# Linear attention with a SwiGLU layer on one core: the first batch's last 64 rows computed with the third batch's attention, one tile cleared earlier, four loads given to the planner first

## The chip, the core and the metric

The kernel runs on one NeuronCore of a Trainium2 chip. Five engines run their own instruction streams and wait for each other through semaphores: TensorE (PE in the profile, with PEld for its weight loads), VectorE (DVE), ScalarE (ACT), GpSimd (POOL) and SyncE (SP), which here only issues DMAs. The metric is the device time of one execution in microseconds (us), less is better. The kernel before takes 323.86 us in the median of three runs (323.74 to 324.04).

## The reference

```python
def _attn_ref(q, k, v, g_norm):                       # (8, 8, 576, 64): batch, heads, rows, head size
    kv = np.einsum('bhsd,bhse->bhde', k, v)
    out = np.einsum('bhsd,bhde->bhse', q, kv)
    rms = np.sqrt(np.mean(out * out, axis=-1, keepdims=True) + 1e-06)
    return (out / rms * g_norm)

def _moe_ref(x, w_gate, w_val, w_out, rms_g):         # x: (4608, 512), d_ff = 1536
    rms = np.sqrt(np.mean(x * x, axis=-1, keepdims=True) + 1e-06)
    xn = x / rms * rms_g
    g = xn @ w_gate
    return (g / (1.0 + np.exp(-g)) * (xn @ w_val)) @ w_out
```

Attention has no softmax: per head a 64 x 64 matrix k^T v is formed from all 576 rows, and every row of q is multiplied by it. So a row of q needs nothing of the other rows, only its batch's k^T v. The two normalisations are fused into one factor per row and head ("the chain": sums of squares, plain and weighted with the gains, then an inverse root).

## The kernel before

**Tiling.** 576 rows of a batch are four chunks of 128 rows (NC = 4) and a remainder of 64 (REM). The rows of the expert layer are worked on in nine groups of 512: the four chunks of each of the eight batches, and one group made of the eight remainders (`xr`), which comes next to last. A group runs 12 blocks of d_ff (NF = 12), each a gate product with silu on ScalarE and a value product multiplied in by VectorE (`gate_of`, `val_of`), four matmuls of 512 columns each; then 48 matmuls with w_out.

**The front.** The first batch is written out by hand, since nothing hides its latency. TensorE spins on a tile of zeros (`idle`, 18 + 4 matmuls) until k and v have landed; k^T v is formed, chunks 0 and 1 are taken through attention, and the first group's first half (256 of 512 rows) starts. Behind its slots `behind(n)` puts the attention of chunks 2 and 3 and of the remainder, n being the place in `early`. Weights arrive meanwhile in eight blocks, issued by GpSimd (gate and value columns of three blocks of d_ff each, `wg0, wv0, ... wv3`), on the same DMA engines as q, k and v; the first group's half uses them in that order. Behind them in GpSimd's queue stand the casts of q's chunks 2 and 3 and of q's remainder (`cast_main`, `cast_rem`), the loads of the second batch, w_out, and the third batch's k and v.

**The later batches.** Each batch's attention runs beside the expert layer of the group before it. A planner (`Placer`) keeps a list of slots: per group 24 slots of gate and value products in turn, then 16 of w_out; 28 slots of the first group's second half stand ahead, so the second group begins with slot 28. Each piece of work has an engine and an estimated cost in us (0.68 a VectorE reduction, 1.2 a GpSimd square, 0.85 a GpSimd load issue). `put` takes the first slot behind the work it depends on at which the engine's backlog stays within a limit (GpSimd 2.0, VectorE and ScalarE 0.9). A slot takes off what it has room for: GpSimd 0.85 in a gate or value slot, VectorE 0.95 in a gate and 0.3 in a value slot. `at` puts work into a slot without asking. In a slot, the other engines' work is emitted ahead of the slot's own product, in the order in which it was placed, and TensorE's behind it. Every engine runs its stream in that order.

**One attention** (`place_attention`, batches 3 to 8): SP turns q by DMA transposition (`qT_dma`: chunks, then remainder); k^T v on TensorE (`kv_mm`) and its copies on VectorE; the products of the four chunks (`o_heads`) and of the remainder (`o_mm`). For each of the five pieces then: a square and a copy on ScalarE (`sq_`, `outa_`), a weighted square on GpSimd (`wsq`), two reductions on VectorE (`red`: of the plain and of the weighted square); the chain in parts on VectorE, a scaling for each piece on VectorE (`xna_`), and transpositions by DMA on SP (`x_dma`) into the next group's x. "Chunk" below counts these pieces from 0. While the second group runs, the third batch's attention, the folding of the gains into the weights (on VectorE and ScalarE), and the loads of the fourth batch (`loads_kv(3)`, slots 39 to 42) are all placed in it; those loads are put in place after the attention.

**Tiles that matter.** `kvs` holds k^T v of two heads each, with zero blocks off the diagonal; two buffers taken in turn by batch. `qTs` is turned q, likewise two. Where a piece has 64 rows, the other 64 are zeroed once by a memset.

Of the kernel before, what the change touches and what calls it, by code (L numbers as in the profile page):

```python
# [87 lines left out]
def kernel(  # L88
# [17 lines left out]
    NC = 4  # L106
# [28 lines left out]


    ident = consts.tile([128, 128], BF16, name="ident")
    gbc = consts.tile([128, D], FP32, name="gbc")
# [21 lines left out]
    for tile_, rows in ((krT, REM // 2), (vr, REM // 2), (rems[0][0], REM)):  # L160
        for r0 in (rows, 2 * rows) if rows < REM else (rows,):
            nc.vector.memset(tile_[r0 : REM if r0 < REM else 128], 0.0)
    idle = consts.tile([128, MAIN], BF16, name="idle")
    nc.vector.memset(idle, 0.0)  # L164
    nc.vector.memset(diag, 0.0)
# [77 lines left out]
    class Att:  # L243
        def __init__(self, b):
            self.b = b
            self.kv, self.qT = kvs[b % 2], qTs[b % 2]
            if b < 2:
                self.qTj = self.qT.rearrange("p c j t -> p (c j t)").rearrange("p (j c t) -> p j c t", j=NS, c=NC + 1)
            else:
                self.qTj = self.qT.rearrange("p c j t -> p j c t")  # L250
            self.kv_chunks = range(NC + 1)
            self.o, self.outa, self.sq = {}, {}, {}
            self.xT = {}
            self.st = None
# [79 lines left out]
        def qT_dma(self):  # L334
            flat = mains[self.b, 0].rearrange("p c h d -> p (c h d)")
            nc.sync.dma_start_transpose(out=self.qT[:, 0:NC].rearrange("p c j t -> p (c j) t"), in_=flat)
            rem = rems[0][self.b % 2][:REM].rearrange("p h d -> p (h d)")
            return nc.sync.dma_start_transpose(out=self.qT[:, NC, :, 0:REM], in_=rem)

        def o_mm(self, c, pool=None):  # L340
            self.o[c] = o = (pool or att_p).tile([128, H, D], FP32, name={None: "att"}.get(pool, "mm1" if pool is mm1_p else "o2"))
            for j in range(NS):
                nc.tensor.matmul(  # L343
                    o[:, 2 * j : 2 * j + 2, :], lhsT=self.qTj[:, j, c, :], rhs=self.kv[:, j, :, :],
                    start=j == 0, stop=j == NS - 1, skip_group_check=True,
                )
# [14 lines left out]
        def part(self, t, n):  # L361

            if n == NC:
                return t[:, NC]
            return t[:, n // 2 * 2 : n // 2 * 2 + 2, n % 2 : H : 2]
# [11 lines left out]
        def xna_pairs(self, o, js, c0, c1):  # L377
            if not hasattr(self, "xna"):
                self.xna = xna_p.tile([128, NC + 1, H, D], BF16, name="xna")
            h0, h1 = 2 * js[0], 2 * js[-1] + 2  # L380
            nc.vector.tensor_tensor(
                out=self.xna[:, c0:c1, h0:h1], in0=o,
                in1=self.al[:, c0:c1, h0:h1].to_broadcast([128, c1 - c0, h1 - h0, D]), op=OP.mult,
            )

        def o_of(self, c):
            return self.o[c] if c == NC else self.o["main", c].rearrange("p c h d -> p (c h) d")

# [59 lines left out]
        def red(self, c, which):  # L448
            if self.st is None:
                self.st = stat.tile([128, 2, NC + 1, H], FP32, name="st")  # L450
            of = self.sq[c][:, which]
# [4 lines left out]
        def chain_t(self):  # L456
            if not hasattr(self, "al"):
                t = lambda n, dt=FP32, h=H: stat.tile([128, NC + 1, h], dt, name=n)
                self.u, self.r, self.t, self.z, self.nt, self.al = (t(n) for n in ("u", "r", "t", "z", "nt", "al"))
                self.s = stat.tile([128, NC + 1], FP32, name="srow")  # L460
                self.y = t("y", I32)
# [55 lines left out]
        def xna_(self, c, eng, src=None):  # L517
            if not hasattr(self, "xna"):
                self.xna = xna_p.tile([128, NC + 1, H, D], BF16, name="xna")
            if src is None and c < NC:  # L520
# [55 lines left out]
        def x_dma(self, c0, c1):  # L576
# [3 lines left out]
            else:  # L580
                to = xr[:, :, self.b * REM : (self.b + 1) * REM]
                of = self.xna[:REM, c0].rearrange("p h d -> p (h d)")
# [13 lines left out]
    def place_attention(P, b, casts=(), at=0, chain_at=0):  # L596
        a, start = Att(b), at + 2
        V, A = nc.vector, nc.scalar
        N1 = range(NC + 1)
        P.floor = max(P.floor, at)  # L600
# [6 lines left out]
        for c in N1:  # L607
            p = P.psum(0.24, lambda: a.o_mm(NC), kv + qt) if c == NC else main
            s = P.put("ACT", 0.6, lambda c=c: a.sq_(c), [p])
            outs[c] = P.put("ACT", 0.6, lambda c=c: a.outa_(c), [p])  # L610
            if c >= 2:
                P.tiles[-1 if c == NC else c - 4] += [s, outs[c]]
            assert outs[c][1] < start + 2 * NF, (b, outs)
# [4 lines left out]
        for n in range(0, 13, 4):  # L618
            prev = [P.put("DVE", 0.8, lambda n=n: [f() for f in a.chain(0, NC + 1)[n : n + 4]], prev, chain_at)]
        xn = [P.put("DVE", 0.68, lambda c=c: a.xna_(c, V), prev + [outs[c]]) for c in N1]  # L620
        put = [P.put("SP", 0.0, lambda c=c: a.x_dma(*c), [xn[c[1] - 1]]) for c in ((0, 2), (2, 4), (4, 5))]
        return put[2 if b == B - 1 else 1][1] + X_SLOTS
# [274 lines left out]

    steps = {6: (0, 3), 7: (3, 5), 8: (5, 8), 9: (8, 10), 10: (10, 12)}

    def behind(n):  # L900
        if n == 0:
            ps = a.qT_mm(ALL, (2, 3))
            a.qT_out(ps[:, 0:2], P0, 2, V)
            a.qT_out(ps[:, 2:4], P1, 2, V)
        elif n == 1:
            a.qT_out(a.qT_mm(ALL, (NC,)), ALL, NC, A)
        elif n in (2, 3):
            js = (P0, P1)[n - 2]
            a.sqT_(a.oT_mm(js, 2, 4, o2_p), js, 2, 4)
        elif n == 4:  # L910
            a.sqT_(a.oT_mm(ALL, NC, NC + 1, o2_p), ALL, NC, NC + 1)
        elif n == 5:
            a.st = None
            a.stat_pairs(P0, 2, 4, att_p, "att")
            a.stat_pairs(P1, 2, 4, att_p, "att")
        elif n == 6:
            a.stat_pairs(ALL, NC, NC + 1, att_p, "att")
        if n in steps:
            for f in a.chain(2, NC + 1)[slice(*steps[n])]:
                f()  # L920
        if n in (8, 9):
            held[n - 8] = a.o_pairs((P0, P1)[n - 8], 2, 4, att_p, "att")
        elif n == 10:
            held[2] = a.o_pairs(ALL, NC, NC + 1, o2_p, "o2")
        if n in (12, 13):
            i = (12, 13).index(n)
# [3 lines left out]
        if n in (15, 16):  # L930
            i = (15, 16).index(n)
# [30 lines left out]
    casts = ()  # L962
    for b in range(1, B):
        if b == 1:
            end = place_second(P, 9)
# [51 lines left out]
```

## Time and profile before

| | us |
|---|---|
| median of three runs | 323.86 |
| the profiled execution's own time | 323.98 |
| its span in the trace | 322.2 |
| TensorE busy | 313.7 (97%) |
| VectorE busy | 175.4 (54%) |
| ScalarE busy | 142.9 (44%) |
| GpSimd busy | 89.0 (28%) |
| first product of the first group's expert layer | 18.55 |
| second group | 58.8 to 93.2 |

Times in the trace count from the start of the span. A row of the timeline has the start, the time taken (of all merged instructions), the engine, the line of the kernel, the operation, what is written and read, how many instructions, and in brackets how long the engine stood idle just before and what ended that. A row of the chain has start, duration and what. A row of DMA issues has the number of issues, the size of one and the time from issue to landing; queue rows have packets, MB and the packets' time as a share of 16 DMA engines (over 100% where packets overlap). L238 are the spins, L677 the gate and value products, L695 the product with silu, L454 the reductions, L446 the weighted squares.

### The profile page before, as it was taken

The page shows a single profiled execution, that of the slowest core. Times are in us where ns is not written, and L with a number is a line of the kernel's source. Part 1 is how long each engine was busy: PE and PEld are TensorE (multiplying, and loading weights), DVE is VectorE, ACT ScalarE, POOL GpSimd, SP SyncE. Part 2 cuts the span into 40 slices and gives each one's busy share as a digit, 9 for nine tenths or more (in the row PEclk, how much of TensorE's full clock was granted, in tenths as well). Part 3 has the DMA queues.
Part 4 walks back from the last instruction along what each step waited for, and adds up shares of the span by engine and source line. Part 5 has one row for each costly group of instructions (what it writes and reads, how often), then busy time and mean ns, then how long its engine had stood idle before and what let it go on. Part 6 is the DMA issues. An engine that isn't in the chain of part 4 may idle for free.

```text
span 322.2 us, 5618 instructions
## 1 busy us (share of the span) xinstructions
PE 313.7 (97%) x2158; PEld 160.0 (50%) x2158; DVE 175.4 (54%) x394; ACT 142.9 (44%) x267; POOL 89.0 (28%) x110
## 2 busy tenths in 40 slices
PE   5999999999999999999999999999999999999995
PEld 1678866544444444444444444444444444444443
DVE  4558437487938671768176917781678133203410
ACT  1375466486659322932283227422742233223321
POOL 8763330039006700670058005800420000000000
PEclk9999999999999999999999999999999999999999
DMA  8999999959664994598559956798000600040002
GB/s 213 220 200 199 194 221 220 220 146 144 139 162 130 124 162 141 145 122 144 150 160 102 141 149 181 90 136 167 36 1 0 171 35 0 1 110 22 0 33 100
DMA packets 78358, 40.51 MB, mean 126 GB/s; under 512 B 41976, under 2 KB 73852, under 8 KB 78332
## 3 DMA queue, kind: packets, MB, share of 16 engines
q0 software_dynamic: 30672, 14.16, 34.5%
q1 hardware_dynamic: 46176, 25.01, 31.4%
q10 hardware_dynamic: 1484, 0.99, 1.0%
q8 instruction: 17, 0.28, 0.4%
q14 instruction: 9, 0.07, 0.1%
HBM read 37.78 MB, written 9.44 MB: 147 GB/s over the span
## 4 chain that ended last, share of the span: by engine, by line
PE 97%; DVE 1%; ACT 1%; issue 0%
PE mm L677 58%; PE o L712 27%; PE mm L238 3%; PE att L275 2%; PE mm L712 2%; PE att L343 1%; PE o L356 1%; PE att L552 1%; PE mm L291 0%; PE att L356 0%; PE mm L739 0%; PE o L739 0%; PE mm L705 0%; PE att L321 0%; ACT sqT L415 0%
## 5 line engine op out<-in xcount | busy, mean ns | idle before, releaser
L695 DVE TENSOR_TENSOR h<-silu,mm 128x512 bf16<-128x512 bf16 (+1 forms) x120 | 75.6, 631 | 83.0 <-PE mm L677 73.7
L686 ACT ACTIVATE silu<-mm 128x512 bf16<-128x512 f32 (+1 forms) x120 | 66.4, 557 | 84.2 <-PE mm L677 77.1
L677 PE MATMUL mm<-x,wv 128*128 128x512 bf16 (+1 forms) x432 | 99.9, 356 | 0.0
L677 PE MATMUL mm<-x,wg 128*128 128x512 bf16 (+1 forms) x420 | 98.5, 358 | 0.5 <-DVE h L695 0.5
L712 PE MATMUL o<-wo,h 128*128 128x512 bf16 x396 | 90.1, 379 | 0.0
L446 POOL TENSOR_TENSOR sq<-sq,g 128x512 bf16<-128x512 bf16 x30 | 34.3, 1153 | 130.2 <-ACT sq L391 130.1
L677 PEld LDWEIGHTS <-wv 128*128 128x128 bf16 x480 | 46.2, 98 | 45.2
L677 PEld LDWEIGHTS <-wg 128*128 128x128 bf16 x468 | 45.0, 98 | 45.4 <-issue 1.0
L712 PEld LDWEIGHTS <-h 128*128 128x128 bf16 x420 | 40.2, 98 | 46.0 <-DVE h L695 0.2
L728 ACT COPY osb<-o 128x512 f32<-128x512 f32 x33 | 19.2, 586 | 69.1 <-PE o L712 69.1
L454 DVE TENSOR_REDUCE st<-sq 128x8 f32<-128x512 bf16 x60 | 38.4, 677 | 1.8 <-POOL sq L446 1.7
L304 DVE CAST kvs<-att 64x256 bf16<-64x256 f32 x14 | 5.9, 422 | 30.0 <-PE att L275 29.8
L521 DVE TENSOR_TENSOR xna<-outa,al 128x512 bf16<-128x512 bf16 x24 | 15.0, 684 | 0.0
L238 PE MATMUL mm<-idle 128*128 128x512 bf16 x27 | 8.7, 493 | 4.0 <-DVE idle L164 4.0
L677 PE MATMUL mm<-xr,wg 128*128 128x512 bf16 x48 | 12.3, 379 | 0.0
L677 PE MATMUL mm<-xr,wv 128*128 128x512 bf16 x48 | 12.3, 379 | 0.0
L209 POOL CAST main_q<-stg 128x1024 bf16<-128x1024 f32 (+1 forms) x12 | 11.3, 970 | 0.4 <-DMA stg<-in_q_dram 0.4
L391 ACT ACTIVATE sq<-att 128x512 bf16<-128x512 f32 x18 | 11.1, 618 | 0.0
L395 ACT CAST outa<-att 128x512 bf16<-128x512 f32 x18 | 10.9, 604 | 0.0
L834 ACT ACTIVATE wv<-wv,gain 128x384 bf16<-128x384 bf16 x16 | 9.0, 608 | 0.4 <-PE mm L677 0.4
L195 POOL DMA_DIRECT2D vc<-in_v_dram x9 | 7.8, 864 | 1.8 <-PE mm L677 1.8
L238 PEld LDWEIGHTS <-idle 128*128 128x128 bf16 x31 | 3.6, 119 | 8.6 <-DVE idle L164 4.0
(139 smaller groups left out, 195.3 us busy)
## 6 DMA issues: line engine op xcount, KB each, us to landing
out_dram<-osb SPq DMA_DIRECT2D x31, 256.0 KB, 2.6
stg<-in_q_dram SPq DMA_DIRECT2D x6, 1024.0 KB, 6.8
vc<-in_v_dram POOLq DMA_DIRECT2D x7, 512.0 KB, 8.0
kc<-in_k_dram POOLq DMA_DIRECT2D x7, 512.0 KB, 6.2
wg<-in_moe_w_gate_dram POOLq DMA_DIRECT2D x4, 384.0 KB, 15.8
wv<-in_moe_w_val_dram POOLq DMA_DIRECT2D x4, 384.0 KB, 17.1
wo<-in_moe_w_out_dram POOLq DMA_DIRECT2D x4, 384.0 KB, 13.1
out_dram<-osb SPq DMA_DIRECT2D x9, 128.0 KB, 2.3
```

The costliest lines, as they stand in the source:

```text
L209: return copy(out=mains[b, t][:, cs[0] : cs[1], h0:h1, :], in_=staged[b, t].rearrange("p h (c d) -> p c h d", c=NC)[:, cs[0] : cs[1], h0:h ...
L238: nc.tensor.matmul(ps, lhsT=idle[:, :128], rhs=idle[:, : ps.shape[-1]], start=True, stop=True, skip_group_check=True)
L391: nc.scalar.activation(out=self.sq[c][:, 0], in_=self.o_of(c), func=ACT.Square)
L395: nc.scalar.copy(out=self.outa[c], in_=self.o_of(c))
L446: eng.tensor_tensor(out=self.sq[c][:, 1], in0=self.sq[c][:, 0], in1=g2, op=OP.mult)
L454: nc.vector.reduce_sum(out=self.part(self.st[:, which], c), in_=of, axis=AX.X)
L521: return eng.tensor_tensor(out=self.part(self.xna, c), in0=self.outa[c].rearrange("p (c h) d -> p c h d", c=2), in1=self.part(self.al, c). ...
L677: nc.tensor.matmul(ps[:, : c1 - c0], lhsT=w[n][:, s, jj * 128 : (jj + 1) * 128], rhs=x_of(g, s, c0, c1), start=s == 0, stop=s == NS - 1)
L686: nc.scalar.activation(out=sis[g, j][:, c0:c1], in_=ps, func=ACT.Silu)
L695: nc.vector.tensor_tensor(out=hs[g, j][:, c0:c1], in0=sis[g, j][:, c0:c1], in1=v_ps, op=OP.mult)
L712: nc.tensor.matmul(ps, lhsT=hs[g, j][:, t * 128 : (t + 1) * 128], rhs=wo[j // OB][:, j % OB, :], start=j == 0, stop=j == NF - 1)
L728: (eng.copy if eng is nc.scalar else eng.tensor_copy)(out=o, in_=ps)
```

## The change

Four things are changed together.

- `idle` is cleared by VectorE's first memset, ahead of those of `krT`, `vr` and `rems`. The memsets of the two q remainder tiles' unused rows fall away.
- The first batch's remainder is taken out of `behind` (turning, products, sums, chain columns, scaling, turning back), and its load on SP and cast on GpSimd out of the front. The remaining steps for chunks 2 and 3 get other places.
- The remainder is loaded by GpSimd with a cast (`q0r`), behind w_out; SP turns it with the third batch's q (`q0T`); and the third batch's attention has a sixth chunk, `o_mm(5)`, which multiplies it by the first batch's k^T v, kept in a third buffer `kvs[2]`. Squares, reductions, the chain (6 x 8 columns instead of 5 x 8), scaling and a transposition into the first batch's place in `xr` follow as for the other chunks.
- The fourth batch's four k and v loads are put into slots 39 to 42 before the third batch's attention is placed, not after it.

Cut to its core:

```diff
+    idle = consts.tile([128, MAIN], BF16, name="idle")
+    nc.vector.memset(idle, 0.0)
...
-    kvs = [consts.tile([128, NS, 2, D], BF16, name=f"kvs{n}") for n in range(2)]
+    kvs = [consts.tile([128, NS, 2, D], BF16, name=f"kvs{n}") for n in range(3)]
+    q0r = consts.tile([REM, H, D], BF16, name="q0r")
+    q0T = consts.tile([128, NS, 128], BF16, name="q0T")
...
-            self.kv, self.qT = kvs[b % 2], qTs[b % 2]
+            self.kv, self.qT = kvs[b % 2 if b else 2], qTs[b % 2]
+            self.chunks = NC + 1 + (b == 2)
...
+            if self.b == 2:
+                nc.sync.dma_start_transpose(out=q0T[:, :, 0:REM], in_=q0r.rearrange("p h d -> p (h d)"))
             return nc.sync.dma_start_transpose(out=self.qT[:, NC, :, 0:REM], in_=rem)
...
+                q_, kv_ = (self.qTj[:, j, c, :], self.kv) if c <= NC else (q0T[:, j, :], kvs[2])
                 nc.tensor.matmul(
-                    o[:, 2 * j : 2 * j + 2, :], lhsT=self.qTj[:, j, c, :], rhs=self.kv[:, j, :, :],
+                    o[:, 2 * j : 2 * j + 2, :], lhsT=q_, rhs=kv_[:, j, :, :],
...
-        N1 = range(NC + 1)
+        N1 = range(a.chunks)
...
-    load_rem(0, 0)
...
-    G.memset(rems[0][1][REM:], 0.0)
+    G.memset(kvs[0], 0.0)
...
-    cast_rem(0, 0, G)
...
     wo_loads = [load_wo(n) for n in range(NF // OB)]
+    G.dma_start(out=q0r, in_=q[0, :, MAIN:S, :].rearrange("h p d -> p h d"))
+    G.memset(q0T, 0.0)
...
-    steps = {6: (0, 3), 7: (3, 5), 8: (5, 8), 9: (8, 10), 10: (10, 12)}
+    steps = {5: (0, 4), 7: (4, 6), 8: (6, 8), 9: (8, 12)}
...
-        elif n == 1:
-            a.qT_out(a.qT_mm(ALL, (NC,)), ALL, NC, A)
...
-        elif n == 4:
-            a.sqT_(a.oT_mm(ALL, NC, NC + 1, o2_p), ALL, NC, NC + 1)
...
-        elif n == 6:
-            a.stat_pairs(ALL, NC, NC + 1, att_p, "att")
...
-        elif n == 10:
-            held[2] = a.o_pairs(ALL, NC, NC + 1, o2_p, "o2")
...
-        elif n == 15:
-            a.xna_pairs(held[2], ALL, NC, NC + 1)
...
-        elif n == 18:
-            a.xT_mm(ALL, (NC,))
-            for j in ALL:
-                a.xT_out(j, (NC,), A)
...
+    G.memset(qTs[0][:, NC, :, REM:], 0.0)
...
+        if b == 2:
+            for n, f in enumerate(loads_kv(b + 1)):
+                P.at("POOL", 0.85, f, starts[1] + 11 + n)
...
-            for n, f in enumerate(loads_kv(b + 1)):
-                if b == 2:
-                    P.at("POOL", 0.85, f, starts[1] + 11 + n)
-                else:
-                    P.put("POOL", 0.85, f, at=starts[b - 1] + 14)
+            for f in loads_kv(b + 1) if b > 2 else ():
+                P.put("POOL", 0.85, f, at=starts[b - 1] + 14)
```

More of the change, by code (lines that the diff above doesn't have):

```diff
@@ L159 @@
     xr = consts.tile([128, NS, MAIN], BF16, name="xr")
[L160 to L164, printed above, removed]
+    for tile_ in (krT, vr):
+        for r0, r1 in ((REM // 2, REM), (REM, 128)):
+            nc.vector.memset(tile_[r0:r1], 0.0)
     nc.vector.memset(diag, 0.0)
@@ L361, in part @@
         def part(self, t, n):
-            if n == NC:
-                return t[:, NC]
+            if n >= NC:
+                return t[:, n]
             return t[:, n // 2 * 2 : n // 2 * 2 + 2, n % 2 : H : 2]
@@ L378, in xna_pairs @@
             if not hasattr(self, "xna"):
-                self.xna = xna_p.tile([128, NC + 1, H, D], BF16, name="xna")
+                self.xna = xna_p.tile([128, NC + 2, H, D], BF16, name="xna")
             h0, h1 = 2 * js[0], 2 * js[-1] + 2
@@ L449, in red @@
             if self.st is None:
-                self.st = stat.tile([128, 2, NC + 1, H], FP32, name="st")
+                self.st = stat.tile([128, 2, NC + 2, H], FP32, name="st")
             of = self.sq[c][:, which]
@@ L457, in chain_t @@
             if not hasattr(self, "al"):
-                t = lambda n, dt=FP32, h=H: stat.tile([128, NC + 1, h], dt, name=n)
+                t = lambda n, dt=FP32, h=H: stat.tile([128, NC + 2, h], dt, name=n)
                 self.u, self.r, self.t, self.z, self.nt, self.al = (t(n) for n in ("u", "r", "t", "z", "nt", "al"))
-                self.s = stat.tile([128, NC + 1], FP32, name="srow")
+                self.s = stat.tile([128, NC + 2], FP32, name="srow")
                 self.y = t("y", I32)
@@ L518, in xna_ @@
             if not hasattr(self, "xna"):
-                self.xna = xna_p.tile([128, NC + 1, H, D], BF16, name="xna")
+                self.xna = xna_p.tile([128, NC + 2, H, D], BF16, name="xna")
             if src is None and c < NC:
@@ L618, in place_attention @@
         for n in range(0, 13, 4):
-            prev = [P.put("DVE", 0.8, lambda n=n: [f() for f in a.chain(0, NC + 1)[n : n + 4]], prev, chain_at)]
+            prev = [P.put("DVE", 0.8, lambda n=n: [f() for f in a.chain(0, a.chunks)[n : n + 4]], prev, chain_at)]
         xn = [P.put("DVE", 0.68, lambda c=c: a.xna_(c, V), prev + [outs[c]]) for c in N1]
-        put = [P.put("SP", 0.0, lambda c=c: a.x_dma(*c), [xn[c[1] - 1]]) for c in ((0, 2), (2, 4), (4, 5))]
+        put = [P.put("SP", 0.0, lambda c=c: a.x_dma(*c), [xn[c[1] - 1]]) for c in ((0, 2), (2, 4), (4, 5), (5, 6))[: a.chunks - 2]]
         return put[2 if b == B - 1 else 1][1] + X_SLOTS
@@ L915, in behind @@
             a.stat_pairs(P1, 2, 4, att_p, "att")
-        elif n == 6:
-            a.stat_pairs(ALL, NC, NC + 1, att_p, "att")
         if n in steps:
-            for f in a.chain(2, NC + 1)[slice(*steps[n])]:
+            for f in a.chain(2, NC)[slice(*steps[n])]:
                 f()
-        if n in (8, 9):
-            held[n - 8] = a.o_pairs((P0, P1)[n - 8], 2, 4, att_p, "att")
-        elif n == 10:
-            held[2] = a.o_pairs(ALL, NC, NC + 1, o2_p, "o2")
-        if n in (12, 13):
-            i = (12, 13).index(n)
+        if n in (7, 8):
+            held[n - 7] = a.o_pairs((P0, P1)[n - 7], 2, 4, att_p, "att")
+        if n in (11, 12):
+            i = (11, 12).index(n)
             a.xna_pairs(held[i], (P0, P1)[i], 2, 4)
-        elif n == 15:
-            a.xna_pairs(held[2], ALL, NC, NC + 1)
-        if n in (15, 16):
-            i = (15, 16).index(n)
+        elif n in (14, 15):
+            i = (14, 15).index(n)
             a.xT_mm((P0, P1)[i], (2, 3), None if i else o2_p)
```

9 lines of the change are left out of this document (5 added, 4 removed).

## The prediction

> **What bounds the kernel now.** I read the page's busy shares and chain first, then the chain in order of time, then the timeline of the two places that the change touches (the front, and the second group's expert layer, where the third batch's attention runs), last the DMA view by issue and by stretch.
>
> ```profile
> span 322.2 us, 5618 instructions
> PEclk9999999999999999999999999999999999999999
> PE 97%; DVE 1%; ACT 1%; issue 0%
> ```
>
> TensorE's instructions are 97% of the chain that ends last. So a matmul taken out pays its full spacing, unless the data of the next one are late; work on the other engines pays only where it ends such a wait. Two stretches decide. The front and the first half of the first group, from the chain in order of time (start, us, what):
>
> ```profile
> 20.75 0.22 PE att L310 x4
> ...
> 22.72 0.22 PE o L404 x4
> ...
> 24.01 0.08 PE att L429 x4
> ...
> 26.31 0.22 PE o L371 x4
> ...
> 30.59 0.19 PE att L552 x4
> ```
>
> The five small pieces are the first batch's remainder on TensorE (turned, multiplied, its sums, the product, turned back). The page's chain has no gap here, but what TensorE reads comes in just ahead of it. The last two weight blocks, DMA issues with their time to landing, and the instructions that issue and first use the last:
>
> ```profile
> wg<-in_moe_w_gate_dram POOLq DMA_DIRECT2D x1, 384.0 KB, 18.1
> wv<-in_moe_w_val_dram POOLq DMA_DIRECT2D x1, 384.0 KB, 18.7
> 10.56 0.74 POOL L228 DMA_DIRECT2D wg<-in_moe_w_gate_dram  x1 [0.92 <-DMA vc<-in_v_dram]
> 11.96 0.74 POOL L229 DMA_DIRECT2D wv<-in_moe_w_val_dram  x1 [0.66 <-DMA vc<-in_v_dram]
> 30.67 0.33 PEld L677 LDWEIGHTS <-wv 128*128 128x128 bf16 x4
> ```
>
> They land at 10.56 + 18.1 = 28.66 and 11.96 + 18.7 = 30.66; the first weight load from the last block starts at 30.67. The transfers, 2.0 apart, keep pace with TensorE exactly, so at 30.67 there is a second bound beside TensorE.
>
> The other stretch is the one place behind 20 us where the chain leaves TensorE:
>
> ```profile
> 76.95 1.03 PE L677 MATMUL mm<-x,wv 128*128 128x512 bf16 x4
> 77.17 0.69 DVE L454 TENSOR_REDUCE st<-sq 128x8 f32<-128x512 bf16 x1 [0.85 <-POOL sq L446]
> 77.77 0.68 DVE L695 TENSOR_TENSOR h<-silu,mm 128x512 bf16<-128x512 bf16 x1
> 78.50 1.02 PE L677 MATMUL mm<-x,wg 128*128 128x512 bf16 x4 [0.53 <-DVE h L695]
> 97.75 17.27 PE mm L677 x80
> ```
>
> In plain flow a matmul takes 17.27/80 = 0.216, so the gate at 78.50 was due at 76.95 + 4 x 0.216 = 77.81: 0.69 lost. It waits for block 8's product (77.77), which stands on VectorE behind a reduction that waited 0.85 for GpSimd's weighted square. GpSimd is late for this reason:
>
> ```profile
> 70.50 1.15 POOL L446 TENSOR_TENSOR sq<-sq,g 128x512 bf16<-128x512 bf16 x1 [1.17 <-ACT sq L391]
> 71.59 0.94 POOL L195 DMA_DIRECT2D kc<-in_k_dram  x1
> ...
> 75.97 2.27 POOL L446 TENSOR_TENSOR sq<-sq,g 128x512 bf16<-128x512 bf16 x2
> ```
>
> The four issues of the fourth batch's k and v, of which the first is shown, stand among the five squares: from 71.59 to 75.97 is 4.38, less the one square between them 3.23. The planner placed squares and reductions before it knew of them.
>
> **Part 1: the zero tile first.** The spinning matmuls wait for it.
>
> ```profile
> 3.66 0.27 DVE L164 MEMSET idle<- 128x256 uint32 x1
> 3.99 7.45 PE L238 MATMUL mm<-idle 128*128 128x512 bf16 x22 [3.99 <-DVE idle L164]
> ...
> 9.08 1.86 PEld L238 LDWEIGHTS <-idle 128*128 128x128 bf16 x9 [0.28 <-issue]
> 18.55 1.31 PE mm L705 x12
> ```
>
> Ahead of it stand five memsets, the first from 0.91 on. At their head it is done at 0.91 + 0.27 = 1.2, and the 22 spins run from 1.25 instead of 3.99, ending at 8.7 instead of 11.44. The first real products cannot follow at once: GpSimd's waits at 10.56 and 11.96, quoted above, end with the landing of the two halves of v, so TensorE idles from 8.7 to 10.5 and has 0.9 to 0.95 in hand behind it. The memsets that move behind only lose 0.27 and are read by the products alone, some 9 us later.
>
> **Part 2: the remainder out of the front.** TensorE drops 0.22 + 0.22 + 0.08 + 0.22 + 0.19 = 0.93. Its copies, squares and chain columns on VectorE and ScalarE lie beside TensorE and count nothing. With part 1 TensorE would reach the last weight block 1.84 to 1.88 earlier. But the block must have landed. What moves its landing is the transfer that leaves, the remainder of q: 64 x 8 x 256 bytes = 0.131 MB in 512 packets. From the DMA view, SP's queue in the stretch from 16 to 20 us (packets, MB, share of 16 engines) and all packets and GpSimd's queue from 20 to 28 us, between them GpSimd's wait for that transfer, and last the chain's row of the third batch's k^T v:
>
> ```profile
> q1 hardware_dynamic: 548, 0.14, 26.0%
> 19.45 0.61 POOL L216 CAST remq<-rstg 64x512 bf16<-64x512 f32 x1 [1.56 <-DMA rstg<-in_q_dram]
> DMA packets 2158, 1.62 MB, mean 203 GB/s; under 512 B 63, under 2 KB 2157, under 8 KB 2157
> q0 software_dynamic: 2157, 1.61, 130.7%
> 63.26 0.75 PE att L275 x40
> ```
>
> By bytes it held up the weights for 0.131 MB / 203 GB/s = 0.65. By packets: 26.0% of 4 us x 16 engines over 548 is 30 ns each, 512 make 15.5, over 16 engines at 1.307 abreast 0.74. I take 0.70: landing at 29.96. With 0.08 allowed from landing to use (an estimate; the row at 30.67 shows 0.01), the use moves from 30.67 to 30.04: **-0.63**. The earlier blocks move alike and bind less. Bounds: no effect if the freed time goes to other packets (0), the whole 1.84 if the landing is no bound. Below nothing would need the next batch's loads, which GpSimd issues some 2 us earlier since it no longer waits for the remainder and casts it (1.56 + 0.61), to pass the weights on their queue; with them outstanding from 20 us on, the last two blocks still came 2.0 apart, which for 0.393 MB is 197 GB/s, the whole rate. So I exclude it.
>
> The new load of the remainder stands behind w_out in GpSimd's queue (one issue, some 0.7, and 0.7 of DMA time), with a memset behind it. The third batch's k and v queue behind both and are first read at 63.26 (last row), so the whole rest of the first group hides it. On SP one more transposition stands ahead of the first group's stores, which no engine waits for. All this counts nothing; without its cover it would cost its own 1 to 2 us once.
>
> **Part 3: the loads placed first.** By the planner's rule the four loads (0.85 each) fill GpSimd's room of slots 39 to 42 of the joint list; chunk 2's square (1.2) would make its backlog 2.4, over 2.0, and moves from slot 41 to 43; the squares of chunks 3, 4 and 5 follow in 44, 46 and 47, and each weighted reduction after its square. GpSimd then: first load in the 1.17 before chunk 1's square at 70.50, that square to 71.65, three loads (3.23 - 0.94 = 2.29) to 73.9, squares ending 75.1, 76.3, 77.4, 78.6 (1.15 each). VectorE, 0.60 from one to the next when busy (77.17 to 77.77): weighted reduction of chunk 3 at 76.3, block 8's product at 76.9, done at 77.6. The gate is now due at 77.81 + 0.22 (part 4) = 78.03, so it waits for nothing: **-0.69**. Bounds: all of it, or none if VectorE is 0.4 or more later than reckoned, since the same wait then stands again.
>
> **Part 4: the sixth chunk.** Four matmuls, as the fifth's:
>
> ```profile
> 69.11 0.22 PE att L343 x4
> ```
>
> **+0.22**, no cover. On VectorE two reductions and a scaling (3 x 0.60), on ScalarE two copies, on GpSimd one square. VectorE after the gate above: chunk 4's two reductions, block 9's product at 78.7, done 79.4, gate 11 due at 78.03 + 8 x 0.216 = 79.76: 0.36 to spare. Late next is the third batch's transposed x, with the time that a transposition takes to land:
>
> ```profile
> 85.60 1.89 DVE L521 TENSOR_TENSOR xna<-outa,al 128x512 bf16<-128x512 bf16 x3
> x<-xna SPq DMA_TRANSPOSE x2, 3.3
> 93.23 1.03 PE L677 MATMUL mm<-x,wg 128*128 128x512 bf16 x4
> ```
>
> Chunk 3's scaling ended at 87.49. Chunk 4's last reduction comes 0.87 earlier (78.1 instead of 77.77 + 2 x 0.60 = 78.97), but two reductions (1.2) and three weight foldings (0.23 each) come in between: 88.5. Issue at 88.7, landing 3.3 later at 92.0; the group is due at 93.23 - 0.69 + 0.22 = 92.76. It fits by 0.76 where it had 2.3.
>
> **Sum**, on the profiled execution's own 323.98 (span 322.2 and 1.78 around it): -0.63 - 0.69 + 0.22 = -1.10, 322.88. The median of the runs shown is 0.12 below that execution, so 322.75.
>
> **Rivals.** *The weights do not hold TensorE back* (their landing moves by more than 1.8): -1.84 - 0.69 + 0.22 gives 321.55. For it, no idle time is charged to a weight; against it, the landing at 30.66 fits the first use to 0.01. *The stall in the third batch stays*, since VectorE has more to do there: 322.75 + 0.69 = 323.45. For it, the sixth chunk's 1.2 of reductions against 0.36 to 0.44 to spare. *The x of the third batch is late*: each us over the 0.76 costs one; 1 us late is 323.0, 2 us 324.0.
>
> *Slower: the matmul clock falls back in the new idle time.* The granted clock reads full in every slice (the page's second row above), but nine spins' weight loads from 9.08 on take 1.86, 0.21 each, where the spins before them took (9.08 - 3.99)/12 = 0.42: TensorE needed 5.1 us of work to get its full pace. If 8.7 to 10.5 without work undoes that, the front's matmuls double: if it stays down for as long as it first did, 5.1 us, they lose half of it, 2.55; if until the first gates at 18.55, the 7.1 from 11.44 on hold about 4 of matmuls by the chain, and they lose 4; minus the 1.2 by which TensorE would have waited for weights anyway: up to +2.8, 322.75 + 2.8 = 325.55. It decides the sign once more than 1.2 + 1.1 = 2.3 of matmul work runs at half pace. Against it, the gap is 1.8, a third of the 5.1. The Trainium skill (TensorE: Matmul & The Clock Gate, Part 1: The HAM clock gate) has the pace fall back after an idle window of about 3.4 us, counted in windows that run freely; by that rule 1.8 is too short and the time stays at 322.75. No run here shows such a gap yet.
>
> **Chances.** Forecast 0.52 (its own range 322.3 to 323.2), weights no bound 0.10, stall stays 0.20, late x 0.08, clock 0.10. The range is 321.5 to 323.9: it takes in the first rival's time and the stall that stays, and leaves out most of the clock and the worst of the late x. A measurement of this kernel tells about 0.2% (0.65) from no change; the line is 323.2. Faster: 0.50 + 0.10 + 0.04 of the stall in part + 0.03 = 0.67; within 0.2%: 0.24; slower: 0.09, the clock and the far end of the late x.
>
> **What would show it.** Spins from about 1.25; the first twelve products near 10.5, still 0.056 apart (0.11 would be the clock); the first load from the last value block at 30.0, with the small waits for weights on the way; GpSimd's four load issues ahead of chunk 2's square; gate 10 with no gap; x landing about 0.7 before its use. I am wrong if the last block is used before 29.5 or after 30.5, if a wait for a product stands anywhere in the second group, or if the spacing of the front's matmuls doubles.

## The result and the profile after

Beside each other the kernel before took 323.96 us (323.74 to 324.04, six runs) and the changed one 322.66 (322.24 to 323.05, six runs): a ratio of 0.996 with an interval of 0.9948 to 0.9973, faster by 0.40%. A second time, beside its last variants, the changed kernel took 322.49 (322.27 to 322.70, five runs) against 324.15, 0.995 (0.9937 to 0.9962). The profiled execution took 322.91 (span 321.1), 1.07 less than the one before.

The page of the changed kernel, its span, the granted clock by slices of 8 us, and the shares of the chain:

```profile
span 321.1 us, 5589 instructions
PEclk9799999999999999999999999999999999999999
PE 95%; DMA 3%; ACT 0%; issue 0%; POOL 0%; DVE 0%; POOLq 0%
```

Two things are new: the clock of the second slice reads 7, and a DMA has 3% of the chain. Both belong to the front. The timeline of TensorE there, with the last group of the spins' weight loads:

```profile
1.19 6.26 PE L240 MATMUL mm<-idle 128*128 128x512 bf16 x22 [1.19 <-DVE idle L138]
4.05 2.90 PEld L240 LDWEIGHTS <-idle 128*128 128x128 bf16 x14 [0.17 <-issue]
10.35 0.38 PE L294 MATMUL mm<-vc,main_k 128*128 128x128 bf16 x4 [2.90 <-DMA vc<-in_v_dram]
10.68 0.55 PE L294 MATMUL mm<-vc,main_k 128*128 128x128 bf16 x4
```

The spins begin at 1.19; fourteen of the 22 load their weights in the 2.90 from 4.05 on, 0.21 each, and only the eight before are slow. The full pace came after 2.9 us of spinning where it had taken 5.1, so the spins end at 7.45, and TensorE stands idle for 2.90. The first four products at 10.35 take 0.38, the next four at 10.68 take 0.55. The stretches of this time (length, busy us of PE, PEld, DVE, ACT, POOL with their counts, granted clock, DMA share, GB/s):

```profile
10.00:10.50 0.50, 0.15 (x3) 0.15 (x3) 0.07 (x1) 0.08 (x1) 0.00 (x0) 1.00 1.47 201
10.50:11.00 0.50, 0.50 (x10) 0.50 (x9) 0.50 (x1) 0.00 (x0) 0.41 (x1) 0.76 1.44 198
13.00:14.00 1.00, 1.00 (x11) 0.94 (x9) 0.25 (x3) 0.00 (x0) 0.94 (x3) 0.50 1.22 245
14.00:15.00 1.00, 1.00 (x9) 0.68 (x7) 1.00 (x3) 0.65 (x2) 1.00 (x3) 0.91 1.22 242
```

The clock is still full when work returns, falls about 0.4 later, and stays at 0.50 until shortly after 14. By the means, 0.76 over half a us and 0.91 over one, from about 10.76 to 14.18, 3.4 us. The chain in order of time shows what that did:

```profile
19.15 1.31 PE mm L712 x12
...
29.00 7.98 PE mm L684 x72
...
73.21 0.22 PE att L349 x4
73.43 7.77 PE mm L684 x36
81.20 9.71 PE o L719 x45
```

The first gate products start at 19.15, not 18.55: 0.60 later instead of some 0.95 earlier. The last two weight blocks (issues with their time to landing, the instruction that issues the last, the queue of SP in the stretch from 16 to 20 us), and the weight loads around its first use:

```profile
wg<-in_moe_w_gate_dram POOLq DMA_DIRECT2D x1, 384.0 KB, 17.2
wv<-in_moe_w_val_dram POOLq DMA_DIRECT2D x1, 384.0 KB, 17.9
11.81 0.74 POOL L231 DMA_DIRECT2D wv<-in_moe_w_val_dram  x1 [0.38 <-DMA vc<-in_v_dram]
q1 hardware_dynamic: 12, 0.00, 0.4%
29.41 0.64 PEld L684 LDWEIGHTS <-wg 128*128 128x128 bf16 x6
30.06 0.96 PEld L684 LDWEIGHTS <-wv 128*128 128x128 bf16 x8
30.27 1.47 PE L684 MATMUL mm<-x,wv 128*128 128x256 bf16 x12
```

SP's 548 packets of this stretch are down to 12, and the last block lands at 11.81 + 17.9 = 29.71. TensorE's weight load comes 0.35 after it, with no wait in brackets, and the first product at 30.27: in this execution TensorE itself is the bound, because of the slow 3.4 us.

The second group. GpSimd's stream, then TensorE's products around the old stall, and last SP's transposition of the third batch's x with the group that reads it:

```profile
70.06 1.15 POOL L452 TENSOR_TENSOR sq<-sq,g 128x512 bf16<-128x512 bf16 x1 [0.29 <-ACT sq L397]
71.16 0.73 POOL L193 DMA_DIRECT2D kc<-in_k_dram  x1
71.88 0.89 POOL L197 DMA_DIRECT2D vc<-in_v_dram  x1
72.77 0.69 POOL L193 DMA_DIRECT2D vc<-in_v_dram  x1
73.47 4.53 POOL L452 TENSOR_TENSOR sq<-sq,g 128x512 bf16<-128x512 bf16 x4
76.72 1.03 PE L684 MATMUL mm<-x,wv 128*128 128x512 bf16 x4
77.58 1.03 PE L684 MATMUL mm<-x,wg 128*128 128x512 bf16 x4
78.45 1.03 PE L684 MATMUL mm<-x,wv 128*128 128x512 bf16 x4
88.43 1.29 SPq L590 DMA_TRANSPOSE x<-xna  x1
92.25 1.03 PE L684 MATMUL mm<-x,wg 128*128 128x512 bf16 x4
```

All four loads (the first, at 68.82, isn't shown) stand ahead of chunk 2's square, four squares follow in one piece, and the gate at 77.58 comes 0.86 after the value product, with no wait. x, issued at 88.43 and 3.3 on its way, lands at 91.73, 0.52 before its use at 92.25, and holds nothing up.

Where the 1.07 came from, by two marks, the first product with the last weight block and the second group's first product with w_out. In the chain of the kernel before, the second mark is

```profile
82.18 9.71 PE o L712 x45
```

and the first is 30.67. So 0.40 was won up to the first mark (30.67 to 30.27), 0.58 between the marks (51.51 to 50.93), and 0.09 behind them.

### The profile page after: what moved, and what is told of

Its sections match the earlier page's. It is cut to its first block, busy times and chain, and to the rows that moved or that the text cites. A ratio compares the mean times of both kernels' runs of the same rounds, so it can differ in the third digit from the quotient of the medians.

```text
span 321.1 us, 5589 instructions
## 1 busy us (share of the span) xinstructions
PE 313.1 (98%) x2142; PEld 160.3 (50%) x2142; DVE 177.2 (55%) x395; ACT 142.2 (44%) x263; POOL 90.9 (28%) x113
## 4 chain that ended last, share of the span: by engine, by line
PE 95%; DMA 3%; ACT 0%; issue 0%; POOL 0%; DVE 0%; POOLq 0%
PE mm L684 58%; PE o L719 27%; DMA vc<-in_v_dram 3%; PE att L278 2%; PE mm L719 2%; PE mm L294 1%; PE att L349 1%; PE o L362 1%; PE att L558 1%; PE att L362 0%; PE mm L746 0%; PE o L746 0%; PE mm L712 0%; PE att L313 0%; PE att L324 0%; ACT sqT L421 0%
## 5 line engine op out<-in xcount | busy, mean ns | idle before, releaser
L452 POOL TENSOR_TENSOR sq<-sq,g 128x512 bf16<-128x512 bf16 x31 | 35.4, 1150 | 127.6 <-ACT sq L397 127.6
L460 DVE TENSOR_REDUCE st<-sq 128x8 f32<-128x512 bf16 x62 | 39.7, 677 | 0.2
L240 PE MATMUL mm<-idle 128*128 128x512 bf16 x27 | 7.5, 439 | 1.2 <-DVE idle L138 1.2
L719 PE MATMUL mm<-wo,h 128*128 128x512 bf16 x24 | 7.8, 379 | 0.0
```

The costliest lines, as they stand in the source:

```text
L452: eng.tensor_tensor(out=self.sq[c][:, 1], in0=self.sq[c][:, 0], in1=g2, op=OP.mult)
L460: nc.vector.reduce_sum(out=self.part(self.st[:, which], c), in_=of, axis=AX.X)
L719: nc.tensor.matmul(ps, lhsT=hs[g, j][:, t * 128 : (t + 1) * 128], rhs=wo[j // OB][:, j % OB, :], start=j == 0, stop=j == NF - 1)
```

## The experiments

"The time behind the first mark" is a profiled execution's time less its first mark. Before: 323.98 - 30.67 = 293.31; after: 322.91 - 30.27 = 292.64. It tells what happened behind the front. Each kernel's time is the median of its runs. The experiments ran on three chips, on which the kernel before took 324.05 (31 spins, zero tile late, both on the loads), 323.95 (zero tile alone, transfer, sixth chunk, small operation) and 324.15 (the last four), so a difference of 0.1 to 0.2 across them tells nothing.

**More spins, so that TensorE doesn't idle.**

```diff
-    spin(mm1_p.tile([128, MAIN], FP32, name="mm1"), 18)
+    spin(mm1_p.tile([128, MAIN], FP32, name="mm1"), 31)
```

> The changed kernel with 31 spins of the zero tile in place of 18 (and the 4 behind them as before), so that TensorE does not stand idle from 7.4 to 10.35 us. Theory A (the idle stretch lets the matmul clock fall, and the halved matmuls of 10.7 to 14.5 are what makes TensorE late at the last weight block): granted clock 1.00 from 8 to 16 us, first gate near 18.55 - 0.95 = 17.6, first load from the last value block at its landing, about 29.75 instead of 30.06; median 0.3 to 0.6 below the changed kernel's 322.66, about 322.2, with all runs within 0.3 of each other. Theory B (the weights' landing alone sets the early part, as the prediction had it): the clock is restored, but the median stays within 0.15 of 322.66.

322.37 (322.27 to 323.10); the clock of all five runs is at least 0.999. The timeline of the weight loads:

```profile
28.90 0.32 PEld L684 LDWEIGHTS <-wg 128*128 128x128 bf16 x3
29.59 1.21 PEld L684 LDWEIGHTS <-wv 128*128 128x128 bf16 x12 [0.37 <-DMA wv<-in_moe_w_val_dram]
```

With the clock kept, TensorE reaches the last block early and waits for its landing. So the weights are the second bound that the prediction took them for. The first mark is 29.60, the time behind it 292.67, as in the changed kernel: its slow clock cost only what stands ahead of the first mark, here 0.67.

**The zero tile cleared late again.**

```diff
-    idle = consts.tile([128, MAIN], BF16, name="idle")
-    nc.vector.memset(idle, 0.0)
...
+    idle = consts.tile([128, MAIN], BF16, name="idle")
+    nc.vector.memset(idle, 0.0)
```

> The changed kernel with the zero tile cleared behind the other memsets again (parts 2 to 4 of the change alone). Theory A: spins end near 11.1, no idle stretch, no fall of the clock, first gate near 18.4, TensorE would reach the last value block at about 30.67 - 0.93 = 29.7, just at its landing; median about 322.3, so clearing the tile first costs 0.3 or more. Theory B (the earlier start of the front is worth its 0.9 or is free): 322.66 or more, up to 323.2.

322.51 (322.20 to 322.76), between what the two theories expected: nothing is lost without part 1. The weight loads:

```profile
28.10 1.21 PEld L684 LDWEIGHTS <-wg 128*128 128x128 bf16 x12 [0.16 <-DMA wg<-in_moe_w_gate_dram]
30.01 0.99 PEld L684 LDWEIGHTS <-wv 128*128 128x128 bf16 x10 [0.70 <-DMA wv<-in_moe_w_val_dram]
```

TensorE waits 0.70 for the last block even so. What part 1 hands to the front ends in front of a landing that it doesn't move.

**The zero tile cleared first, alone, in the kernel before.** 
```diff
+    idle = consts.tile([128, MAIN], BF16, name="idle")
+    nc.vector.memset(idle, 0.0)
...
-    idle = consts.tile([128, MAIN], BF16, name="idle")
-    nc.vector.memset(idle, 0.0)
```

> The kernel before with the zero tile cleared first and nothing else changed. TensorE is there only 0.01 behind the last weight block, so nothing can be gained. Theory A (the idle stretch sometimes halves the clock for 3.4 us): executions with a granted clock of 0.995 come out 0.4 to 0.9 above the kernel before, 324.4 to 324.9, those with a full clock at 323.7 to 324.1. Theory B (the fall of the clock costs nothing because the weights are waited for anyway): all within 0.2 of the kernel before, 324.0.

324.36 (323.60 to 324.84) against 323.95: no gain. The eleven runs part by the granted clock of the execution: five with 0.993 or 0.994 took 324.36 to 324.55, five of the six others 323.60 to 324.09. The sixth, at 324.84, is the profiled one: in it the last block was first used at 31.57, 0.90 later than before, at full clock. So part 1 by itself gains nothing that these runs show, and loses about 0.5 where the clock falls.

**The four loads placed last again.**

```diff
-        if b == 2:
-            for n, f in enumerate(loads_kv(b + 1)):
-                P.at("POOL", 0.85, f, starts[1] + 11 + n)
...
-            for f in loads_kv(b + 1) if b > 2 else ():
-                P.put("POOL", 0.85, f, at=starts[b - 1] + 14)
+            for n, f in enumerate(loads_kv(b + 1)):
+                if b == 2:
+                    P.at("POOL", 0.85, f, starts[1] + 11 + n)
+                else:
+                    P.put("POOL", 0.85, f, at=starts[b - 1] + 14)
```

> The changed kernel with the fourth batch's loads placed after the third batch's attention again. Theory A (the order of planning took away the 0.69 stall): the wait for a weighted square returns between blocks 7 and 10 of the second group, 0.7 or more with a sixth chunk behind it; median 0.6 to 1.2 above the changed kernel's 322.66, 323.3 to 323.9. Rival (the stall went because work shifted by the earlier front, not because of the order): no wait over 0.2 in the second group, median within 0.2 of 322.66.

323.22 (323.00 to 323.38), 0.56 more than the changed kernel, a little under the range expected. In four of its seven runs the clock fell; at full clock alone the means are 323.09 and 322.36, 0.73 apart. The old stall is back, in VectorE's and TensorE's timeline:

```profile
76.39 0.69 DVE L460 TENSOR_REDUCE st<-sq 128x8 f32<-128x512 bf16 x1 [0.85 <-POOL sq L452]
77.00 0.68 DVE L702 TENSOR_TENSOR h<-silu,mm 128x512 bf16<-128x512 bf16 x1
77.73 1.02 PE L684 MATMUL mm<-x,wg 128*128 128x512 bf16 x4 [0.31 <-DVE h L702]
```

The gate was due at 76.39 + 4 x 0.216 = 77.25 (a value product started at 76.39 too) and came at 77.73: 0.48 lost, where the kernel before lost 0.69. That is 0.21 less, which fits the sixth chunk's four matmuls: they delay the gate by 0.22, and the product that it waits for was due no later.

**The four loads placed first, alone, in the kernel before.** 
```diff
+        if b == 2:
+            for n, f in enumerate(loads_kv(b + 1)):
+                P.at("POOL", 0.85, f, starts[1] + 11 + n)
...
-            for n, f in enumerate(loads_kv(b + 1)):
-                if b == 2:
-                    P.at("POOL", 0.85, f, starts[1] + 11 + n)
-                else:
-                    P.put("POOL", 0.85, f, at=starts[b - 1] + 14)
+            for f in loads_kv(b + 1) if b > 2 else ():
+                P.put("POOL", 0.85, f, at=starts[b - 1] + 14)
```

> The kernel before with the fourth batch's loads placed first and nothing else changed. Theory A: the 0.69 stall before block 10's gate in the second group goes, nothing else moves; 323.96 - 0.69 = 323.27. Rival (the stall goes only in company with the other parts, or moves to another product): 323.7 to 324.1.

323.28 (323.00 to 323.72, nine runs) against 324.05, a ratio with the interval 0.9965 to 0.9984: 0.77 saved. Part 3 does by itself what the prediction took for it. The profiled execution, at 323.71, is one of the two slowest: there the front is 0.35 later than before (first mark 31.02), while the time behind the mark is 292.69, 0.62 less than before. The front is late there by itself: a small operation of VectorE (the gain product, of which more below) takes 2.04 where it took 0.52, and stands on the chain. The last block had landed at 30.54, so TensorE was the bound.

**The transfer back in the front.** To the kernel with 31 spins, SP's load of the first batch's remainder returns at its old place; nothing reads it.

```diff
+    load_rem(0, 0)
...
-    spin(mm1_p.tile([128, MAIN], FP32, name="mm1"), 18)
+    spin(mm1_p.tile([128, MAIN], FP32, name="mm1"), 31)
```

> The changed kernel with 31 spins and with the remainder's 0.131 MB load back on SP behind q's chunks 2 and 3, into a tile that nothing reads (its other load stays). Theory A (the last weight block's landing is the bound of the front, and that load is what delays it): landing near 30.6 instead of 29.53, first weight load from it at once behind; median 0.7 to 1.1 above the 322.37 of 31 spins alone, 323.1 to 323.4. Rival (TensorE's own work sets the front): median within 0.2 of 322.37.

323.74 (323.62 to 323.99, eleven runs), 1.37 more than without it and above the range expected. The weight load:

```profile
30.47 1.21 PEld L684 LDWEIGHTS <-wv 128*128 128x128 bf16 x12 [0.74 <-DMA wv<-in_moe_w_val_dram]
```

One transfer of 0.131 MB moved this use by 0.88 (29.59 to 30.47), or by 0.78 against a second profile with 31 spins (29.69, below), while TensorE's work stayed as it was. That is the weight term measured by itself, 0.1 to 0.2 more than the 0.70 of the prediction. The other 0.48 lies behind the mark (293.15 against 292.67), though between the marks it is the same 50.95: the span ends 3.0 after VectorE's last copy, in the kernel without the transfer 2.6. What the last store's landing has to do with a load in the front wasn't found out.

**Without the sixth chunk.** On the kernel with 31 spins. The first batch's remainder is left out of the attention: its 64 rows enter the expert layer as zeros.

```diff
-            self.chunks = NC + 1 + (b == 2)
+            self.chunks = NC + 1
...
+    G.memset(xr[:, :, 0:REM], 0.0)
```

> The changed kernel with 31 spins and without the sixth chunk: the first batch's remainder is loaded and turned, but not multiplied, normalised or put into x; its rows of x are set to zero, so its 64 output rows are wrong. The sum's term for it is four matmuls, 0.22: median 322.37 - 0.22 = 322.15. If its work on VectorE, GpSimd and SP still costs something in the second group (a wait for a product, or the third batch's x landing late), more than 0.4 goes: under 321.95.

322.07 (322.00 to 322.27), 0.30 less than with it, of which 0.10 lies ahead of the first mark (29.50 against 29.60). Between the marks it is 50.72 against 50.94, 0.22: four matmuls, and nothing else of the chunk, are on the path.

**Another form of one small operation on VectorE.** The gain product of 128 x 4 elements, in the front, had taken from 0.25 to 2.04 us in these profiles. Here it is written so that the factor comes as a second tensor.

```diff
-    V.tensor_scalar(
-        out=gain, in0=gall[:, 0:NS], scalar1=gcol, scalar2=float(d_model) ** 0.5, op0=OP.mult, op1=OP.mult
+    V.scalar_tensor_tensor(
+        out=gain, in0=gall[:, 0:NS], scalar=float(d_model) ** 0.5, in1=gcol.to_broadcast([128, NS]),
+        op0=OP.mult, op1=OP.mult,
```

> The changed kernel with 31 spins, and VectorE's small gain product (128x4, a tensor_scalar that took 0.52 in some traces and 1.69 to 2.04 in others, each time beside GpSimd's memsets) written as a scalar_tensor_tensor with two tensor inputs. Theory (that instruction at times waits for GpSimd's memsets, and the front behind it is then late by up to 1.4): it takes under 0.7 in the trace, and the runs of 322.85 and 323.10 that 31 spins alone had do not come: all five within 322.1 to 322.5. Rival (that spread comes from something else, as the transfers): spread as before, 322.2 to 323.1.

The operation takes 0.15, but the time is 322.65 (322.52 to 322.87), no better than 322.37. The last block landed at 11.93 + 18.0 = 29.93 and was used at 29.99. The idea that this operation sets the spread of these runs fell: TensorE waits for the weights here (0.21 at the last block), and a faster front buys nothing as long as it does.

**Four variants once more, side by side**: the changed kernel, 24 spins, 31 spins, and the zero tile late. New among them is only

```diff
-    spin(mm1_p.tile([128, MAIN], FP32, name="mm1"), 18)
+    spin(mm1_p.tile([128, MAIN], FP32, name="mm1"), 24)
```

> The changed kernel itself, beside its three variants on the same chip. Theory A (the idle stretch of 1.7 to 2.9 us lets the clock fall in part of the executions): granted clock 0.995 in about half of the runs, those at 322.8 to 323.1, the others at 322.2 to 322.6; median 322.4 to 322.9. Theory B (the clock does not matter): no difference between the two kinds of run.

> The changed kernel with 24 spins instead of 18, which leaves TensorE idle for 0.4 to 1.6 us instead of 1.7 to 2.9. Theory A (the clock falls only after an idle stretch that comes near a 3.4 us window): granted clock 0.998 or more in all runs, median 322.2 to 322.5. Rival (any idle stretch can do it): 0.995 in some runs, which are then 0.4 or more slower.

> 31 spins again. Theory A: granted clock 0.998 or more in all runs; median 322.2 to 322.5, the spread left being the landing of the last weight block. It should be 0.2 to 0.4 below the changed kernel beside it.

> Zero tile late again. Theory A: like 31 spins, 322.3 to 322.6, since both reach the last weight block before it lands; so clearing the tile first is worth nothing by itself, and costs 0.1 to 0.4 against this one where the clock falls. Theory B (an earlier front helps): 0.2 or more above 31 spins in the median.

| | us | first mark | landing of the last block | time behind the mark |
|---|---|---|---|---|
| changed | 322.49 (322.27 to 322.70) | 29.83 | 29.80 | 292.66 |
| 24 spins | 322.44 (322.32 to 322.78) | 29.73 | 29.72 | 292.65 |
| 31 spins | 322.34 (322.32 to 322.40) | 29.69 | 29.66 | 292.65 |
| zero tile late | 322.45 (322.33 to 322.83) | 29.84 | 29.78 | 292.67 |

This time the changed kernel kept its clock in all five runs (0.998 and more), where half were expected to lose it, so these runs say nothing on when it falls. All four kernels are alike: each uses the last block within 0.06 of its landing. Its idle stretch, and that of the kernel with 31 spins:

```profile
10.26 0.38 PE L294 MATMUL mm<-vc,main_k 128*128 128x128 bf16 x4 [1.55 <-DMA vc<-in_v_dram]
```

```profile
1.19 9.42 PE L240 MATMUL mm<-idle 128*128 128x512 bf16 x35 [1.19 <-DVE idle L138]
10.45 0.39 PE L294 MATMUL mm<-vc,main_k 128*128 128x128 bf16 x4
```

1.55 us without work here, none with 31 spins. Over both rounds the changed kernel's eleven runs have a median of 322.51, the ten with 31 spins 322.36: 0.15 less, with a clock that fell in none of them. It may be the better version, but 0.15 is less than the spread of either: two of the ten, 322.85 and 323.10, were slower at full clock, for a reason that wasn't found.

## Why the prediction was right, and where it was not

**The total** held: 322.75 forecast, 322.66 and 322.49 measured. That 322.66 came so near is luck in part: it lies between two kinds of run, with and without a fall of the clock, and none of the six took it.

**Part 1** is the step that failed. It had TensorE idle from 8.7 to 10.5 and put the clock's fall among the rivals. In the profiled execution the spins reached full pace sooner, the gap grew to 2.90, and the clock fell: the spacing of the front's products doubled, which the prediction had named as a sign of being wrong. What was off is the 5.1 us of warming up, taken as a property of the kernel from one execution; from the first spin to the first of the quick weight loads the profiles show 2.8 to 5.9. The price was small for the reason given with the rival: TensorE had a wait for weights ahead of it. The front was 1.55 late against plan at the first gate (0.60 later, not 0.95 earlier). Not all of that is the clock: in TensorE's timeline the first gate starts at 18.99 here, at 18.15 and 17.55 in the two profiles with 31 spins, so 0.84 to 1.44 later. The first mark came only 0.67 and 0.58 after theirs, the rest being eaten by that wait. Of the first six runs of the changed kernel three have a granted clock of 0.995 and took 322.81 to 323.05, mean 322.92; three have 0.998 or more and took 322.24 to 322.51, mean 322.36. So a fall costs 0.56 here, and the sign is safe, as a loss of 1.1 was needed to turn it (the prediction's 2.3 are matmul work at half pace, before the wait takes up 1.2 of it). In the kernel with the loads last it costs 0.22 (means 323.31 and 323.09); why less there wasn't found.

How often: 12 of the 29 runs with the zero tile first and 18 spins ahead of the data (the changed kernel, loads last, and the zero tile first alone) have a clock of 0.995 or less; of the 46 with more spins or a late zero tile none is below 0.997. The Trainium skill (TensorE: Matmul & The Clock Gate, Part 1: The HAM clock gate) has the pace change at free-running windows of 3.4 us. This trace agrees with the length, 3.4 at half pace. It does not agree with a gap under 3.4 being safe, which is how the prediction read it: 2.90 was enough. The four profiled gaps with 18 spins are 2.90, 2.48, 1.67 and 1.55, and only at the first did the clock fall.

The traces show more than the lengths. By the clock records of the profiled execution the full pace begins at 3.94, the clock falls at 10.76 and is back at 14.18. These are 6.83 and 3.41 apart, twice and once the same step, and the step from 7.35 to 10.76 holds the whole gap. The zero tile first alone, with its quick weight loads and the end of its gap:

```profile
5.87 2.08 PEld L238 LDWEIGHTS <-idle 128*128 128x128 bf16 x10 [0.28 <-issue]
10.94 0.38 PE L291 MATMUL mm<-vc,main_k 128*128 128x128 bf16 x4 [2.48 <-DMA vc<-in_v_dram]
```

Its full pace begins at 5.95 in the record, so a step of 3.41 would end at 9.36, inside its gap (8.46 to 10.94), and no step there is idle for more than 1.6. The gaps of 1.67 and 1.55 are cut likewise, at 9.57 and 9.90. So it seems to matter where a gap lies in the steps, and not its length alone. That fits all four profiles, but with one fall among them it isn't shown, and how much of a step must be idle stays open.

**Part 2**: that the weights' landing is the bound right behind TensorE was right, shown by the waits for `wv` in the kernels that get there early. The term was a little small: 0.70 was taken, and in the ten profiles without the transfer the last block lands between 29.44 and 29.97, 0.69 to 1.22 before the old 30.66, while putting it back costs 0.78 to 0.88. The old landing varies too, from 30.41 to 31.50 in the four profiles with the transfer. That the weight load at 30.06 agrees with the forecast 30.04 is chance: landing 0.25 sooner than thought, TensorE 0.35 behind it. In some of these profiles the last of three silus on ScalarE ends within 0.07 of the same landing, and the row of TensorE's product names it. It isn't what TensorE waited for: these products are summed in three tiles used in turn (`mm1_p`), so the first product with the last block needs only the first of the three silus. In the first profile with 31 spins that product starts at 29.60 while the second silu runs until 29.66; in the second profile the first silu is done at 29.01, 0.65 ahead of the landing.

**Part 3** was right: no wait for a product in the second group, GpSimd's order as worked out, the four squares ending at 78.0 (78.6 predicted, of which 0.40 is the earlier front). By itself 0.77, against 0.69. The kernel before has a second, smaller stall at the next gate, which the prediction left out:

```profile
79.36 1.03 PE L677 MATMUL mm<-x,wv 128*128 128x512 bf16 x4
80.29 1.02 PE L677 MATMUL mm<-x,wg 128*128 128x512 bf16 x4
```

The gate comes 0.93 after the value product instead of 0.86, and 0.69 + 0.07 = 0.76 is what was measured. The rival that keeps the stall fell with it.

**Part 4** was right: 0.22 between the marks, and x not late.

**Between the marks** the sum was -0.47, and -0.57 to -0.58 was measured, with another 0.09 behind the second mark. Of these 0.2, 0.07 is that smaller stall, and 0.07 lies at the very end: the span ends 2.57 after VectorE's last copy, not 2.64. The rest is not assigned to any step. The surplus makes up for the lost front: in the profiled execution -0.40 -0.58 -0.09 = -1.07 met -1.10 by way of two errors.

**The rival without a weight bound** (321.55) fell: even with 31 spins TensorE waits for the last block. A kernel as fast as that needs the weights earlier, not more room on TensorE.

## What to carry to other kernels

When work is taken off the path, look for the second bound right behind it, an operand that lands at the same moment: it decides how much of the saving is kept, and it also takes up what goes wrong ahead of it. Spinning matmuls must reach until the data are there; to start them earlier without adding to them opens a gap at their end, whose length differs from run to run (so does the end of a fixed number of them: 31 spins, with the 4 behind them, end at 11.21 in one profile and at 10.61 in the other). Work with fixed slots belongs into a planner's list before the work that it may shift.

## What the runs showed of the hardware

In the one fall that was profiled, the clock fell after work had come back, not in the gap: idle from 7.45 to 10.35, full clock until about 10.76, then 3.4 us at 0.50. The price of the gap stands behind it in the trace.

VectorE's product of 128 x 4 elements took 0.25 to 2.04 us as a TENSOR_SCALAR, always beside GpSimd's memsets of some 0.5 us each; here the longest, from the kernel with the loads first alone, and the form with two tensors:

```profile
13.96 2.04 DVE L862 TENSOR_SCALAR gain<-gall 128x4 f32<-128x4 f32 x1
```

```profile
14.26 0.15 DVE L868 SCALAR_TENSOR_TENSOR gain<-gall 128x4 f32<-128x4 f32 x1
```

The Trainium skill (SBUF — State Buffer, A bandwidth-pool intuition that's wrong) has GpSimd and some VectorE operations exclude each other wholly on a shared port rather than slow each other. The ends fit that: in all thirteen profiles with this form it ends 0.03 after one of the memsets does (the 2.04 us after the last of them, at 15.97), while the form with two tensors ran in the midst of one. No run here took the memsets away.

A transfer of 0.131 MB in 512 packets, at the 203 GB/s of the stretch worth 0.65 by its bytes, held later transfers up by 0.78 to 0.88 in these profiles.
